# Two weight remainders and the output matrix of a decode step, loaded with source runs that span several written rows

## The chip, the cores and the metric

The kernel runs on one core of a Trainium2 chip. The metric is device time in microseconds (us) of one execution. All matrices come from HBM and are read once into SBUF, the core's on-chip memory of 128 partitions; the result goes back to HBM. The core has five instruction queues: TensorE (PE, matrix multiply, with weight loads listed as PEld), VectorE (DVE), ScalarE (ACT), GpSimd (POOL) and SyncE (SP). In this kernel SP issues every transfer, and one hardware queue (q1 in the profile) spreads each of them over the core's 16 DMA engines.

## What is computed

Eight tokens (B = 8, one position each, D = 576) pass through two branches, which a sigmoid gate mixes. The inputs are bfloat16.

```python
g = sigmoid((x * gate_w).sum(-1, keepdims=True))
# a: attention of 32 query heads over 16 key/value heads, the last W = 2048 positions of the caches
q = x @ wq                                             # wq: 576 x 4096
p = softmax(einsum(q, k[:, :, Sk-W:]) * 128 ** -0.5)
a = einsum(p, v[:, :, Sk-W:]).reshape(B, 1, 4096) @ wo # wo: 4096 x 576
# b: layernorm and a two-layer network
h = gelu(layernorm(x) @ w1 + b1)                       # w1: 576 x 4608
b = h @ w2 + b2                                        # w2: 4608 x 576
out = g * a + (1 - g) * b
```

The windows of the two caches are 2 x 67.1 MB; wq, w1, w2 and wo are 4.7, 5.3, 5.3 and 4.7 MB.

## The kernel before, in words

**An order made by a planner.** The kernel registers every operation with an engine, its dependencies, an estimated cost and a priority (`add` and `dma`, line 50 and below). `_Plan.schedule` (line 62) then lays out one order for each engine from these estimates; `emit` writes it out with semaphore waits for the dependencies. On each engine, and on SP, instructions run in that fixed order. An `after=` dependency fixes order alone and makes no wait.

**The buffers.** `RAW` holds four slots of 32 KB a partition, and behind them a fifth, shorter one (number `ND` = 4, 18 KB a partition). The fifth shares its bytes with `KT2`, a work buffer of transposed keys (line 280). `take_slot` (line 606) deals out slots 1, 2, 0, 3 in turn; `slot_free[s]` lists who must have finished reading slot `s` before it is filled again.

**The stream.** First come wq and w1. Each has 576 rows and is split into 512 rows, four to a partition (`d_wqm`, `d_w1m`), and a remainder of 64 rows (`d_wqr`, `d_w1r`, lines 407 and 417), in which each row is cut in two halves so that the 128 halves fill 128 partitions: 4096 bytes a partition for wq, 4608 for w1. Then 16 items of keys and 16 of values follow, 4 MB each (`load_item`, line 613, issued at line 618): 128 partitions of 32 KB, where a source item of one batch and head gives four consecutive partitions. Behind the last value item come w2 and wo:

```python
M_CUTS = [[24], [8, 3, 1]]
stream += [("M", 0), ("W", 0), ("W", 1), ("M", 1)]
```

`M` 0 is 24 of the 36 column blocks of w2 in one transfer (3456 KB), `M` 1 the other 12 in three transfers of 8, 3 and 1 blocks (1152, 432 and 144 KB; `m2_chunk`, issued at line 865). `W` 0 and 1 are the two halves of wo (2304 KB each, 18,432 bytes a partition; `wo_chunk`, line 832, issued at line 836). `W` 0 goes to slot ND and so waits for the last matmuls that read `KT2`, those of the last key item; `W` 1 and both `M` go to slots from `take_slot`. What each waits for: `M` 0 the third-last value item's matmuls, `W` 1 the last key item's transposes, `M` 1 the second-last value item's matmuls.

**Who uses them.** `AccGroup` (line 570) makes the matmuls of the two final products, all at line 579. They add into one PSUM bank; every 576-column block is done as two matmuls of 288 columns, on different parts of the array. `m2_…` groups multiply with w2 and need only hT, the hidden layer, which is ready early. `proj0` and `proj1` multiply with wo and need `oT`, the finished attention output (line 822), whose last part comes from the last value item by way of a short matmul group (`sel_x`, line 819). Between `proj0` and `proj1` stands `fill`: eight matmuls of 512 columns whose result nobody reads (`filler`, line 846, matmuls at line 851 and in the helper at line 175). Groups are tied to each other by `after=`, so that their order in PE's queue follows the stream. At the end VectorE and ScalarE each copy half of the accumulator (lines 900 and 901), and SP writes the output (line 903).

## Time and profile before

| | |
|---|---|
| Device time, median of 3 runs | 364.61 us (364.40 to 364.72) |
| Span of the profiled execution, first to last instruction | 363.0 us (its own total is not shown apart; the runs are about 1.6 us longer than the span) |
| Mean granted TensorE clock | 0.958 of full speed |
| TensorE / VectorE / ScalarE busy | 82% / 64% / 46% of the span |
| Bytes read from HBM | 154.29 MB |
| DMA engines busy with q1 | 98.8% of the span, 16 engines |
| Transfers under 8 KB a packet | 1228 of 6102 packets |

The profile's page gives busy shares, then the span in 40 slices, the DMA queues, and the chain that ended last: the work followed back from the last instruction, at each step to whatever released it. Further views used below are that chain in order of time, the timeline of one engine, the waits, the DMA queue in a stretch of time, and a table of stretches with the busy time of each engine and the granted TensorE clock. Busy time of SP (SPq) is the time in which it issues a transfer; the transfer itself runs long after that.

### The profile page before, as it was taken

To read this page: it belongs to the slowest core of one execution; us is meant where nothing else is said; L and a number is where in the kernel's file an instruction comes from. 1 tells how busy PE (TensorE), PEld (TensorE's weight loads), DVE (VectorE), ACT (ScalarE), POOL (GpSimd) and SP (SyncE) were. 2 spreads that over 40 slices of the span, in tenths; PEclk is the share of its full clock that TensorE was granted. 3 is DMA by queue.
4 is the path that set the end of the run, shared out by engine and by line. 5 is a ranking of instruction groups with operands and counts; after the bars stand their busy time and mean duration, and the time that the engine had idled before them with its cause. 6 is when DMAs were issued, how large, how long until landed. Compare 5 with 4: busy or idle time off the path is not lost.

```text
span 363.0 us, 4821 instructions
## 1 busy us (share of the span) xinstructions
PE 297.9 (82%) x1954; PEld 125.3 (35%) x1423; DVE 231.4 (64%) x166; ACT 168.6 (46%) x130; POOL 22.9 (6%) x52
## 2 busy tenths in 40 slices
PE   0456366999999979998897979997989698999875
PEld 0111000434252615242433417150615152436742
DVE  0452989576666694929385768566675949295720
ACT  1022106656647463663637373838374554656000
POOL 9032030000010000000100000000000000003000
PEclk9976598999999998999999989999999999999999
DMA  8999999999999999999999999999999999999996
GB/s 347 436 437 406 455 412 455 412 455 412 450 415 451 415 451 413 441 426 441 426 441 426 435 430 437 430 437 428 437 430 437 430 435 430 437 430 433 415 430 257
DMA packets 6102, 154.45 MB, mean 426 GB/s; under 512 B 694, under 2 KB 840, under 8 KB 1228
## 3 DMA queue, kind: packets, MB, share of 16 engines
q1 hardware_dynamic: 6092, 154.30, 98.8%
q8 instruction: 8, 0.13, 0.1%
q14 instruction: 2, 0.02, 0.0%
HBM read 154.29 MB, written 0.01 MB: 425 GB/s over the span
## 4 chain that ended last, share of the span: by engine, by line
DMA 56%; DVE 27%; PE 14%; issue 1%; ACT 1%; SPq 0%; POOL 0%
DMA arena<-in_A_k_cache_dram 47%; DVE arena L718 21%; PE ps L175 6%; DMA arena<-in_B_w_dram 6%; DMA arena<-in_A_x_dram 3%; DVE arena L668 2%; PE ps L188 2%; PE ps L755 2%; PE ps L732 2%; DVE arena L645 1%; PE ps L501 0%; PE ps L579 0%; DVE arena L557 0%; DVE arena L521 0%; ACT arena L536 0%
## 5 line engine op out<-in xcount | busy, mean ns | idle before, releaser
L718 DVE STREAM_TRANSPOSE arena<-arena 128x4096 f32<-128x4096 f32 (+1 forms) x34 | 141.7, 4175 | 21.9 <-DMA arena<-in_A_k_cache_dram 21.9
L674 ACT ACTIVATE arena<-arena 32x2048 bf16<-32x2048 bf16 x60 | 114.5, 1908 | 71.4 <-DVE arena L668 42.9
L175 PE MATMUL ps<-arena 128*128 128x512 bf16 (+3 forms) x531 | 136.1, 402 | 0.0
L188 PE MATMUL ps<-arena 128*128 x840 | 109.5, 277 | 7.3 <-issue 1.2
L188 PEld LDWEIGHTS ps<-arena 128*128 x840 | 81.4, 97 | 34.3 <-issue 19.0
L732 PE MATMUL ps<-arena 128*128 128x512 bf16 x128 | 51.4, 401 | 27.6 <-DVE arena L718 26.1
L645 DVE TENSOR_REDUCE arena<-ps 128x1 f32<-128x2048 f32 x16 | 36.7, 2291 | 53.8 <-PE ps L175 53.8
L732 PEld LDWEIGHTS ps<-arena 128*128 128x128 bf16 x128 | 12.5, 98 | 131.7 <-issue 75.3
L649 ACT ACTIVATE arena<-ps,arena 128x2048 bf16<-128x2048 f32 x16 | 40.7, 2543 | 0.5
L646 ACT ACTIVATE arena<-arena 128x1 f32<-128x1 f32 x16 | 3.2, 203 | 63.5 <-DVE arena L645 63.5
L755 PE MATMUL ps<-arena 128*128 128x256 bf16 x184 | 25.3, 272 | 1.1 <-DVE arena L663 1.1
L755 PEld LDWEIGHTS ps<-arena 128*128 128x128 bf16 x184 | 16.9, 99 | 18.8 <-issue 14.6
L668 DVE STREAM_TRANSPOSE arena<-arena 128x1024 f32<-128x1024 f32 x15 | 18.1, 1205 | 2.9 <-ACT arena L649 2.9
L579 PE MATMUL ps<-arena 128*8 128x288 bf16 (+1 forms) x140 | 9.6, 286 | 4.0 <-DMA arena<-in_A_wo_dram 3.3
L739 POOL MEMSET arena<- 128x4096 f32 x1 | 3.5, 3511 | 148.2 <-PE ps L175 148.2
L685 PE MATMUL ps<-arena 128*128 128x512 bf16 x16 | 6.5, 407 | 6.5 <-ACT arena L649 5.2
L629 POOL COPY arena<-arena 32x64 bf16<-32x64 bf16 x16 | 3.7, 229 | 123.3 <-PE ps L175 122.4
L901 ACT ACTIVATE arena<-ps 8x288 bf16<-8x288 f32 x1 | 0.4, 402 | 19.5 <-PE ps L579 19.5
L422 DVE COPY arena<-arena 8x128 bf16<-8x128 bf16 x2 | 0.5, 228 | 13.9 <-DMA arena<-in_A_x_dram 13.9
L579 PEld LDWEIGHTS ps<-arena 128*8 128x8 bf16 (+1 forms) x140 | 5.8, 86 | 9.9 <-DMA arena<-in_A_wo_dram 3.3
L900 DVE CAST arena<-ps 8x288 bf16<-8x288 f32 x1 | 0.4, 446 | 12.3 <-PE ps L579 12.3
L557 DVE TENSOR_TENSOR arena<-arena 128x1152 f32<-128x1152 f32 x1 | 1.4, 1358 | 9.7 <-ACT arena L555 9.7
(106 smaller groups left out, 94.0 us busy)
## 6 DMA issues: line engine op xcount, KB each, us to landing
arena<-in_A_k_cache_dram SPq DMA_DIRECT2D x16, 4096.0 KB, 28.7
arena<-in_A_v_cache_dram SPq DMA_DIRECT2D x16, 4096.0 KB, 25.5
arena<-in_B_w_dram SPq DMA_DIRECT2D x1, 4608.0 KB, 22.0
arena<-in_A_wo_dram SPq DMA_DIRECT2D x2, 2304.0 KB, 23.8
arena<-in_A_wq_dram SPq DMA_DIRECT2D x1, 4096.0 KB, 12.6
arena<-in_B_w_dram SPq DMA_DIRECT2D x1, 3456.0 KB, 24.1
arena<-in_B_w_dram SPq DMA_DIRECT2D x1, 1152.0 KB, 22.3
arena<-in_B_w_dram SPq DMA_DIRECT2D x1, 576.0 KB, 23.0
```

The costliest lines, as they stand in the source:

```text
L175: return e.add_instruction(mybir.InstMatmult(name=nc.get_next_instruction_name(), engine=mybir.EngineType.PE, ins=[e.lower_ap(rhs), e.lowe ...
L188: return e.add_instruction(mybir.InstMatmult(name=nc.get_next_instruction_name(), engine=mybir.EngineType.PE, ins=[rhs, lhsT], outs=[e.low ...
L579: ins = e.matmul(ps[32 * j:32 * j + 8, BK_ACC, 0:JN], lhsT, rhs[:, JN * j:JN * j + JN], start=False, stop=True, skip_group_check=True, til ...
L629: return e.tensor_copy(dst, src)
L645: mx = add("dve", lambda e: e.tensor_reduce(out=k(g, MX + x), in_=scores, axis=AXL.X, op=ALU.max), deps=[qk_unit[t]], name="mx%d" % t, cos ...
L649: ex = add("act", lambda e: e.activation(out=bass.AP(arena, offset=aoffs("P"), ap=[[AST, 128], [64, 32], [1, 2], [2, 32]]), in_=ps[:, 0:4, ...
L668: pc = add("dve", lambda e: e.transpose(view("PC").bitcast(F32), view("P").bitcast(F32)), deps=[ex] + (sp_done[t - 1][0] if t else [o_acc0 ...
L674: return e.activation(out=bass.AP(arena, offset=32 * a * AST + aoffs(home) + 64 * a, ap=[[AST, 32], [256, 32], [1, 64]]), in_=bass.AP(aren ...
L685: mm = e.matmul(*args, start=True, stop=False, skip_group_check=True) if n == 0 else held_matmul(nc, e, *args, start=True, stop=False, ski ...
L718: return e.transpose(bass.AP(arena_f, offset=foffs(base) + 2048 * h0, ap=[[AST // 2, 128], [1, 2048 * nh]]), bass.AP(arena_f, offset=foffs ...
L732: mm = e.matmul(*args, start=False, stop=True, skip_group_check=True) if rc == 0 else held_matmul(nc, e, *args, stop=True, skip=True)
L755: return e.matmul(dst, bass.AP(arena, offset=aoffs(home) + 256 * q + ee, ap=[[AST, 128], [2, 128]]), slot(s).rearrange("p (r k d) -> p r k ...
```

## The change

A new helper, `wide_read`, issues a DMA copy whose two sides have different shapes but the same elements in the same order. Three loads use it.

The remainders of wq and w1 are now described on the HBM side as 16 runs of four whole rows (32,768 bytes for wq, 36,864 for w1), and on the SBUF side as before, 128 rows of 4096 or 4608 bytes: one run fills eight partitions. The bytes land in the same places.

The two halves of wo become one transfer of 128 runs of 36,864 bytes on the HBM side; each run fills two rows of 18,432 bytes in the same partition, one in the slot that `take_slot` gives and one in slot ND. The transfer therefore waits for both slots. The stream's tail is now wo, `M` 0, `M` 1, so wo takes the slot that `M` 0 had, and `M` 0 the one that `W` 1 had. Both `proj` groups wait for the one transfer; `fill` stands behind `proj1`. In PE's order `proj0`, `proj1` and `fill` come first, and all of `M` 0's 48 matmuls behind them; before, 32 of these stood ahead of `sel_x`, 16 behind it, and all 48 ahead of `proj0`. No other instruction changes its place on any engine.

```diff
+def wide_read(nc, e, dst, src):
+    return e.add_instruction(mybir.InstDMACopy(
+        name=nc.get_next_instruction_name(), engine=mybir.EngineType.SP, queue="qSPDynamicHW", mode="Copy",
+        ins=e.lower_ap_dma(src), outs=e.lower_ap_dma(dst), oob_is_err=True, cce_op=ALU.bypass))
...
-        d_wqr = dma("sp", lambda e: e.dma_start(wq_r, A_wq[512:576, :].rearrange("k (s c) -> (k s) c", s=2)), "wq", 64 * 8192, name="d_wqr")
+        d_wqr = dma("sp", lambda e: wide_read(nc, e, wq_r, A_wq[512:576, :].rearrange("(q k) c -> q (k c)", k=4)), "wq", 64 * 8192, name="d_wqr")
...
-        d_w1r = dma("sp", lambda e: e.dma_start(w1_r, B_w1[512:576, :].rearrange("k (s c) -> (k s) c", s=2)), "w1", 64 * F * 2, name="d_w1r", after=[d_w1m])
+        d_w1r = dma("sp", lambda e: wide_read(nc, e, w1_r, B_w1[512:576, :].rearrange("(q k) c -> q (k c)", k=4)), "w1", 64 * F * 2, name="d_w1r", after=[d_w1m])
...
-        stream += [("M", 0), ("W", 0), ("W", 1), ("M", 1)]
+        stream += [("W", 0), ("M", 0), ("M", 1)]
...
-        def wo_chunk(i):
-            s = ND if i == 0 else take_slot()
-            dst = slot(s)[:, 0:WOR * D].rearrange("p (j c) -> p j c", j=WOR)
-            src = A_wo.rearrange("(p j) c -> p (j c)", j=WOP)[:, WOR * D * i:WOR * D * (i + 1)]
-            d = dma("sp", lambda e: e.dma_start(slot(s)[:, 0:WOR * D], src), "s%d" % s, WOR * 128 * D * 2, deps=slot_free[s], name="d_wo%d" % i, after=last_dma[-1:])
-            last_dma.append(d)
-            mms = [(oT[:, WOR * i + j, :], dst[:, j, :]) for j in range(WOR)]
-            slot_free[s] = [AccGroup("proj%d" % i, mms, [oT_done[n] for n in range(NG)] + [d], cost=2.4, prio=2, after=o_m2[-1:]).op]
-            o_m2.append(slot_free[s][0])
-            if i == 0:
-                filler("fill", 8, o_m2[-1:])
+        def wo_both():
+            s = take_slot()
+            homes = (s, ND)
+            dst = bass.AP(arena, offset=aoffs("RAW") + s * DE, ap=[[AST, 128], [(ND - s) * DE, 2], [1, WOR * D]])
+            src = A_wo.rearrange("(p j) c -> p (j c)", j=WOP).unsqueeze(1)
+            d = dma("sp", lambda e: wide_read(nc, e, dst, src), "s%d" % ND, WOP * 128 * D * 2, deps=slot_free[ND] + slot_free[s], name="d_wo", after=last_dma[-1:])
+            last_dma.append(d)
+            for i, h in enumerate(homes):
+                mms = [(oT[:, WOR * i + j, :], slot(h)[:, j * D:(j + 1) * D]) for j in range(WOR)]
+                slot_free[h] = [AccGroup("proj%d" % i, mms, [oT_done[n] for n in range(NG)] + [d], cost=2.4, prio=2, after=o_m2[-1:]).op]
+                o_m2.append(slot_free[h][0])
+                if i == 1:
+                    filler("fill", 8, o_m2[-1:])
...
-            {"K": k_item, "V": v_item, "W": wo_chunk, "M": m2_chunk, "B": bias}[kind](i)
+            {"K": k_item, "V": v_item, "W": lambda i: wo_both(), "M": m2_chunk, "B": bias}[kind](i)
```

## The prediction

> **What bounds the kernel now.** I read the page's queue rows first, since every byte is read once: if the queue is full from end to end, only transfer time and the two ends count.

> ```profile
> span 363.0 us, 4821 instructions
> DMA  8999999999999999999999999999999999999996
> q1 hardware_dynamic: 6092, 154.30, 98.8%
> ```

> The DMA digits are 9 in all slices but the first and the last, and q1 keeps 16 engines at 98.8% of the span. So whatever lengthens or shortens a transfer moves the end by as much. The second view is the chain that ended last, in order of time.

> ```profile
> 1.71 12.15 DMA arena<-in_A_x_dram
> ...
> 79.66 25.41 DMA arena<-in_A_k_cache_dram
> ...
> 337.03 22.31 DMA arena<-in_B_w_dram
> ...
> 359.38 1.71 PE ps L579 x24
> ...
> 361.12 0.45 DVE arena L900
> ```

> From 79.66 us on it is nearly all waiting for key transfers; at the end it is the 1152 KB piece of w2, 24 matmuls, the copy out. The tail, where the change reorders work, I read in the timeline of all engines.

> ```profile
> 345.67 2.13 PE L579 MATMUL ps<-arena 128*8 128x288 bf16 x32
> ...
> 347.73 0.19 PE L819 MATMUL ps<-arena 128*128 128x32 bf16 x1
> ...
> 348.33 0.44 DVE L822 TENSOR_TENSOR arena<-ps,arena 128x64 bf16<-128x64 f32 x1 [0.92 <-PE ps L175]
> 351.23 2.13 PE L579 MATMUL ps<-arena 128*8 128x288 bf16 x32 [1.85 <-DMA arena<-in_A_wo_dram]
> ...
> 353.29 0.39 PE L851 MATMUL ps<-arena 128*128 128x512 bf16 x1
> 353.51 1.67 PE L175 MATMUL ps<-arena 128*128 128x512 bf16 x7
> 356.65 2.13 PE L579 MATMUL ps<-arena 128*8 128x288 bf16 x32 [1.46 <-DMA arena<-in_A_wo_dram]
> ...
> 359.38 1.70 PE L579 MATMUL ps<-arena 128*8 128x288 bf16 x24 [0.61 <-DMA arena<-in_B_w_dram]
> ```

> PE takes each weight transfer as it lands: `M` 0 at 345.67, the halves of wo at 351.23 and 356.65, `M` 1 from 359.38. Between the pieces it idles, since the queue is slower than PE. Each of these gaps will matter.

> **The change part by part.** The sum is made on the profiled span, 363.0 us; the runs (median 364.61) lie 1.6 us above it, and a difference is carried over as it is.

> *Fewer, longer reads.* How the time of a packet depends on its size comes from two stretches of the queue: one of key and value rows of 32,768 bytes, one of mostly 9216-byte rows.

> ```profile
> DMA packets 1493, 43.23 MB, mean 432 GB/s; under 512 B 172, under 2 KB 172, under 8 KB 172
> ...
> q1 hardware_dynamic: 1490, 43.19, 100.1%
> ```
> ```profile
> DMA packets 74, 0.61 MB, mean 380 GB/s; under 512 B 8, under 2 KB 8, under 8 KB 8
> ...
> q1 hardware_dynamic: 74, 0.61, 89.7%
> ```

> In the first, 432 GB/s at 100.1% busy is 27.0 bytes/ns for one engine, 1215 ns for a 32 KB packet. In the second, 66 packets above 512 B hold 0.61 MB, 9242 bytes each, at 380/0.897 = 424 GB/s: 349 ns each. The slope is 866 ns over 23,526 bytes, 36.8 ps a byte, which leaves some 9 ns that a packet costs whatever its size. The remainders have 8 rows on each engine (128/16); with one read for eight rows, 7 x 9 = 63 ns go, twice. wo goes from 16 packets on an engine to 8: 72 ns. Together 0.2 us, if the 9 ns belong to the read; if they belong to the written row, nothing. I take 0.18, since the rows count one packet for a read and a write, and keep 0 as the other end. Longer runs do not move faster otherwise: wo's rows already have half the length.

> *Issuing.* The three copies leave the short form of issue.

> ```profile
> 0.80 0.39 SPq L407 DMA_DIRECT2D arena<-in_A_wq_dram  x1
> ...
> 282.81 0.54 SPq L618 DMA_DIRECT2D arena<-in_A_v_cache_dram  x1
> ...
> 321.52 0.33 SPq L865 DMA_DIRECT2D arena<-in_B_w_dram  x1
> 329.90 0.81 SPq L836 DMA_DIRECT2D arena<-in_A_wo_dram  x2
> 337.03 1.28 SPq L865 DMA_DIRECT2D arena<-in_B_w_dram  x3
> ```

> The wq remainder took 0.39 us to issue; key and value loads, whose two sides also differ in shape, 0.54. The queue is empty behind the first load, so its 0.15 us more is on the path: +0.15 (0 if it issues as before). For the other two the queue is full when they issue.

> *wo waits for two slots.* SP's wait at line 836 was 8.0 us, for the last key item's matmuls, until 329.90. Before, `M` 0 had gone out at 321.52; now wo goes first and stands until 329.9, with both `M` behind it.

> ```profile
> SPq L836 <- PE ps L175: 8.0, 1, 8.0
> ```
> ```profile
> arena<-in_B_w_dram SPq DMA_DIRECT2D x1, 3456.0 KB, 24.1
> arena<-in_A_wo_dram SPq DMA_DIRECT2D x2, 2304.0 KB, 23.8
> ```

> What hides this is the last value item. `M` 0 landed at 345.67, and 3456 KB at 432 GB/s are 8.2 us, so the value item moves until 337.5. An issue at 329.9 leaves 7.6 us of cover: cost nothing. Without the cover it would be 8 us. `M` 0 is issued right behind, `M` 1 at 337.03 as before (its wait is unchanged, and 19 us of bytes stand ahead of it).

> *The tail in the new order.* wo is 4608 KB: 10.9 us, landed at 348.4. `sel_x` no longer stands behind `m2` matmuls (until 347.80 before), so oT is ready no later than its 348.77, rather at 348.5; `proj` starts at about 348.6. The 64 `proj` matmuls go in pairs, two parts of the array at once:

> ```profile
> L579 PE MATMUL ps<-arena 128*8 128x288 bf16 (+1 forms) x140 | 9.6, 286 | 4.0 <-DMA arena<-in_A_wo_dram 3.3
> ```

> 32 of them took 2.13 us, one lasts 0.286: 15 steps in 1.84 us, 0.1225 us a pair. So `proj` ends at 348.6 + 32 x 0.1225 = 352.5, and `fill` (353.29 to 355.18 before, 1.9 us) at 354.4. The bytes up to the end of `M` 0 are those that ended with wo before, so `M` 0 lands where the second half of wo did, at 356.6. Then 48 + 24 matmuls are still to do, 36 pairs: the last starts at 356.65 + 35 x 0.1225 = 360.94 and ends at 361.22. Before, the end was 361.08, set by landings (`M` 1's first piece at 359.34, the last one 24 matmuls of 1.71 us later). So PE, not the last landing, ends the kernel: +0.15 us (361.22 for 361.08), at full clock.

> *The clock in that tail.* PE now idles from 354.4 to 356.6, 2.2 us; before from 355.18 to 356.65, 1.46. What a gap of that size does shows in mid-kernel, in the table of stretches (its length, then busy us and instructions of PE, PEld, DVE, ACT and POOL, granted clock, DMA share, GB/s):

> ```profile
> 131.68:135.10 3.42, 1.45 (x7) 0.10 (x1) 3.42 (x1) 3.37 (x3) 0.00 (x0) 1.00 1.04 450
> 135.10:138.51 3.41, 3.16 (x8) 0.40 (x3) 1.23 (x5) 2.60 (x2) 0.00 (x0) 0.50 1.02 442
> 189.70:193.11 3.41, 1.72 (x9) 0.10 (x1) 2.78 (x1) 3.36 (x3) 0.00 (x0) 1.00 1.03 442
> 193.11:196.53 3.42, 3.42 (x19) 0.73 (x8) 0.18 (x1) 2.99 (x3) 0.00 (x0) 1.00 0.95 412
> 353.55:356.96 3.41, 1.95 (x14) 0.25 (x8) 0.00 (x0) 0.00 (x0) 0.00 (x0) 1.00 0.94 400
> 356.96:360.38 3.42, 2.81 (x46) 1.76 (x42) 0.00 (x0) 0.00 (x0) 0.00 (x0) 1.00 0.76 307
> ```
> ```profile
> 132.30 0.84 PE L175 MATMUL ps<-arena 128*128 128x512 bf16 x3
> 135.35 0.61 PE L732 MATMUL ps<-arena 128*128 128x512 bf16 x1 [2.22 <-DVE arena L718]
> 135.76 1.48 PE L175 MATMUL ps<-arena 128*128 128x512 bf16 x3
> ```

> The granted clock changes in steps of 3.41 us. A stretch in which PE was busy 1.45 of 3.42 us (42%, one gap of 2.22) is followed by one at 0.50, in which three matmuls spread over 1.48 us instead of 0.84; a stretch with 1.72 busy (50%) is followed by full clock. So the limit lies between 42 and 50%. From 135.10 on, 64 steps of 3.413 lead to 353.5. In the stretch 353.55 to 356.96 PE was busy 1.95 us (57%). In the new order it holds `fill` until 354.4 and matmuls from 356.6: 1.2 us, 36%. Then 356.96 to 360.38 runs at half clock, and 3.41 us there do 1.7 us of work. The end is 1.7 us later.

> [...]

> If the steps lie elsewhere in another execution, the drop comes when a step holds at least 1.7 to 2.0 us of the 2.2-us gap, and not when PE had already been slowed at 348 (the new hole between 345.6 and 347.5), which lengthens `proj` and closes the gap: by these times a third to a half of the positions.

> Sum: +0.15 issue, −0.18 packets, +0.15 PE at the end, +1.7 half clock = +1.8: 364.61 + 1.8 = 366.4 us.

> **The rivals.** *The tail stays at full clock.* The same sum without the last term: +0.1, 364.7 us. For it: steps in another place, or `fill` a little later (wo landing 0.5 us later than reckoned moves `fill` so that the stretch is over 50% busy). Against it: the place of the steps in this trace.

> *Two engines write into one part of SBUF.* A key or value item gives four consecutive partitions and moves at 432 GB/s although its two sides have unequal outer counts (32 and 128). A new run gives eight. If an engine's eight rows then cross into the part of SBUF that another engine fills at that time, each has half the rate, and the remainders (0.52 + 0.59 MB, 2.6 us at 432 GB/s) take up to twice as long: +1.3 if half of it collides, +2.6 at most; 364.61 + 0.1 + 2.4 = 367.1 us. Nothing in the trace shows a written run of eight partitions, and the full rate of the key loads speaks against it. wo is not touched: its 128 runs stay in their partitions.

> [...]

> *Faster.* The start is slow:

> ```profile
> DMA packets 106, 0.43 MB, mean 310 GB/s; under 512 B 0, under 2 KB 0, under 8 KB 106
> ...
> q1 hardware_dynamic: 106, 0.43, 87.8%
> ```

> In the first 1.4 us the queue moves 310 GB/s instead of 432: 0.4 us lost, and the first packet cannot start before 1.8. If one long read for each engine closes this, the issue is not longer, all 0.2 us of packets go, and PE stays at full clock: −0.4 −0.2 +0.15 = −0.45. It decides, over 0.2%, when a further 0.3 us come from less spread between engines at the end: 363.8 us.

> *The change does not do what it says:* the queue may cut the runs into row-sized packets again. Then the 0.18 stays, and with it the tail: 366.6, or 364.9 at full clock. It changes no sign and goes with those cases.

> **How the numbers follow.** About 0.2%, 0.7 us, is what a measurement of this kernel can tell from no change. Half clock in the tail: 0.36 (the profiled place of the steps gives it surely, a free place in a third to a half). Full clock and no collision: 0.29. Collision: 0.24. Faster by over 0.2%: 0.11. So slower 0.60, same 0.29, faster 0.11. The predicted time is that of the first, 366.4; its own range is 366.0 to 366.8. The range for all reaches from 364.2 (full clock, some of the start gained) to 367.8 (collision with its 2.6 us and some spread); below it lies faster, above it collision and half clock together (up to 369).

> **What would show it.** Packets of 32 KB and more in place of the 256 of 4096 and 4608 bytes; the wq remainder's issue at 0.54; wo landed near 348.4; `fill` ended near 354.4 and PE idle until 356.6; a granted clock of 0.50 in a stretch that begins between 356 and 358.3, with the last 72 matmuls at 0.245 us a pair. The prediction is wrong if the clock stays at 1.00 there; a collision would show as a later landing of x (before, the chain waits for it until 13.86) and of everything behind it, at an unchanged rate in the key loads.

## The result

The changed kernel takes 366.94 us (median of 4 runs, 366.58 to 367.04) against 364.61 us, a ratio of 1.0063 with a 95% interval of 1.005 to 1.0077: 2.3 us slower. The spans of its four executions are 365.3 to 365.4 us; the profiled one before was 363.0. The forecast was 366.4 us, with a range of 364.2 to 367.8. The number came out, but most of it from another cause than the one I had put first; that 366.4 lies so near to 366.94 is luck. One execution in the whole record, the third of `e10` (400.16 us, not traced), lies far above the others of its kernel and is left out of the comparisons.

**The profile after.** First the page: span, DMA engines and rate in 40 slices, packets of the whole run.

```profile
span 365.3 us, 4801 instructions
DMA  8999999999999999999999999999999999999995
GB/s 298 419 401 436 405 456 405 456 409 456 414 443 434 427 452 411 449 413 449 416 452 416 443 427 434 441 423 447 413 449 416 452 414 445 423 438 445 408 437 240
DMA packets 5734, 154.45 MB, mean 423 GB/s; under 512 B 678, under 2 KB 824, under 8 KB 956
```

For comparison, the rate row of the kernel before:

```profile
GB/s 347 436 437 406 455 412 455 412 455 412 450 415 451 415 451 413 441 426 441 426 441 426 435 430 437 430 437 428 437 430 437 430 435 430 437 430 433 415 430 257
```

The packets fell from 6102 to 5734: 224 for the remainders, 128 for wo, and 16 of the small ones (under 512 B: 678 after, 694 before; there is one transfer fewer, but what these packets carry no view says). So the long runs are really read as such. The queue is as full as before (DMA digits of 9), but it moves less in the first three slices: 298 for 347 GB/s, 419 for 436 and 401 for 437. In the first the remainder of wq is loaded, in the third that of w1 begins. From the fourth slice on, up to the last, both rows swing between about 405 and 456.

Next the transfers that matter here, picked from the list, with their size and the time from issue to landing, first after, then before:

```profile
arena<-in_B_w_dram SPq DMA_DIRECT2D x1, 4608.0 KB, 22.5
arena<-in_A_wo_dram SPq DMA_DIRECT2D x1, 4608.0 KB, 18.5
arena<-in_B_w_dram SPq DMA_DIRECT2D x1, 576.0 KB, 24.6
arena<-in_A_wq_dram SPq DMA_DIRECT2D x1, 512.0 KB, 4.6
```
```profile
arena<-in_B_w_dram SPq DMA_DIRECT2D x1, 4608.0 KB, 22.0
arena<-in_B_w_dram SPq DMA_DIRECT2D x1, 576.0 KB, 23.0
arena<-in_A_wq_dram SPq DMA_DIRECT2D x1, 512.0 KB, 3.3
```

And the issues at the start in the timeline of SP (start, duration), after and then the two of w1 before:

```profile
0.80 0.62 SPq L196 DMA_DIRECT2D arena<-in_A_wq_dram  x1
1.49 0.56 SPq L414 DMA_DIRECT2D arena<-in_A_wq_dram  x1
3.65 0.36 SPq L422 DMA_DIRECT2D arena<-in_B_w_dram  x1
4.05 0.52 SPq L196 DMA_DIRECT2D arena<-in_B_w_dram  x1
```
```profile
3.23 0.36 SPq L416 DMA_DIRECT2D arena<-in_B_w_dram  x1
3.63 0.43 SPq L417 DMA_DIRECT2D arena<-in_B_w_dram  x1
```

The 512 KB of wq, issued first, land 4.6 us after the issue for 3.3. The main part of w1 was issued at 3.23 before and at 3.65 now, so it lands at 3.65 + 22.5 = 26.15 for 3.23 + 22.0 = 25.23: 0.9 later. The w1 remainder lands at 4.05 + 24.6 = 28.65 for 3.63 + 23.0 = 26.63: 2.0 later, another 1.1. From there to the last transfer the shift hardly grows, as the chain that ended last shows (start, duration; its first transfer and its end):

```profile
4.61 35.08 DMA arena<-in_A_k_cache_dram
332.74 26.02 DMA arena<-in_B_w_dram
358.80 4.60 PE ps L585 x72
```

`M` 0 lands at 332.74 + 26.02 = 358.76. The forecast put it where the second half of wo had landed, at 356.6; it is 2.2 later, and the end is 2.3 later. So nearly the whole loss was made in the first 29 us. The rate in between is unchanged: 434 GB/s from 140 to 240 us, 432 before.

Last the tail, in PE's timeline (lines picked out) and in the table of stretches (columns as in the prediction: length, busy us of PE, PEld, DVE, ACT, POOL, granted clock, DMA share, GB/s):

```profile
344.17 3.65 PE L761 MATMUL ps<-arena 128*128 128x256 bf16 x32
349.70 0.19 PE L825 MATMUL ps<-arena 128*128 128x32 bf16 x1 [1.88 <-DVE arena L814]
350.82 5.32 PE L585 MATMUL ps<-arena 128*8 128x288 bf16 x64 [0.53 <-DVE arena L828]
356.29 1.67 PE L175 MATMUL ps<-arena 128*128 128x512 bf16 x7 [0.16 <-issue]
358.80 4.58 PE L585 MATMUL ps<-arena 128*8 128x288 bf16 x72 [0.83 <-DMA arena<-in_B_w_dram]
```
```profile
346.54:349.96 3.42, 1.54 (x22) 1.17 (x16) 1.64 (x5) 0.00 (x0) 0.00 (x0) 1.00 0.92 396
349.96:353.37 3.41, 2.88 (x35) 1.60 (x28) 0.44 (x1) 0.00 (x0) 0.00 (x0) 0.50 1.03 446
353.37:356.78 3.41, 3.25 (x49) 1.85 (x41) 0.00 (x0) 0.00 (x0) 0.00 (x0) 1.00 0.94 399
356.78:360.20 3.42, 2.59 (x30) 1.04 (x26) 0.00 (x0) 0.00 (x0) 0.00 (x0) 1.00 0.94 399
360.20:363.61 3.41, 3.18 (x52) 2.10 (x48) 0.19 (x1) 0.19 (x1) 0.00 (x0) 1.00 0.45 178
```

The chain ends with 72 matmuls right behind `M` 0's landing, as forecast, but they take 4.58 us at a granted clock of 1.00. The half-clock stretch is there, only earlier: PE idles from 347.8 to 349.7, waiting for attention's last part; the stretch from 346.54 is 45% busy; the next one runs at 0.50. The 64 `proj` matmuls stretch to 5.32 us, `fill` ends at 358.0, and of the 2.2-us gap ahead of the last 72 matmuls 0.83 us remain. The clock drop fell on work that has slack: the last 72 matmuls wait for `M` 0 all the same.

### The profile page after: what moved, and what is told of

It reads as the page before. It is cut to its first block, busy times and chain, and to the rows that moved or that the text cites. A ratio compares the mean times of both kernels' runs of the same rounds, so it can differ in the third digit from the quotient of the medians.

```text
span 365.3 us, 4801 instructions
## 1 busy us (share of the span) xinstructions
PE 296.5 (81%) x1935; PEld 126.0 (34%) x1423; DVE 231.5 (63%) x166; ACT 168.6 (46%) x130; POOL 23.0 (6%) x52
## 2 busy tenths in 40 slices
DMA packets 5734, 154.45 MB, mean 423 GB/s; under 512 B 678, under 2 KB 824, under 8 KB 956
## 3 DMA queue, kind: packets, MB, share of 16 engines
q1 hardware_dynamic: 5724, 154.30, 98.6%
## 4 chain that ended last, share of the span: by engine, by line
DMA 55%; DVE 22%; PE 20%; SPq 1%; issue 1%
DMA arena<-in_A_k_cache_dram 48%; DVE arena L724 18%; PE ps L175 9%; DMA arena<-in_B_w_dram 7%; PE ps L188 6%; PE ps L738 3%; DVE arena L674 2%; PE ps L585 1%; DVE arena L651 1%; DVE arena L800 1%; PE ps L761 0%; SPq L196 0%; PE ps L691 0%; SPq L414 0%; DVE arena L908 0%
## 5 line engine op out<-in xcount | busy, mean ns | idle before, releaser
L175 PE MATMUL ps<-arena 128*128 128x512 bf16 (+3 forms) x524 | 134.6, 397 | 13.5 <-DVE arena L724 10.6
L738 PE MATMUL ps<-arena 128*128 128x512 bf16 x122 | 48.7, 399 | 19.0 <-DVE arena L724 17.3
L761 PE MATMUL ps<-arena 128*128 128x256 bf16 x184 | 25.3, 273 | 1.2 <-DVE arena L669 1.1
L428 DVE COPY arena<-arena 8x128 bf16<-8x128 bf16 x2 | 0.5, 228 | 15.2 <-DMA arena<-in_A_x_dram 15.2
L691 PE MATMUL ps<-arena 128*128 128x512 bf16 x11 | 4.4, 399 | 5.2 <-ACT arena L655 5.2
L908 DVE CAST arena<-ps 8x288 bf16<-8x288 f32 x1 | 0.4, 445 | 12.7 <-PE ps L585 12.7
## 6 DMA issues: line engine op xcount, KB each, us to landing
arena<-in_B_w_dram SPq DMA_DIRECT2D x1, 4608.0 KB, 22.5
arena<-in_B_w_dram SPq DMA_DIRECT2D x1, 3456.0 KB, 26.0
arena<-in_B_w_dram SPq DMA_DIRECT2D x1, 576.0 KB, 24.6
```

Of the source, the lines that this page charges most:

```text
L175: return e.add_instruction(mybir.InstMatmult(name=nc.get_next_instruction_name(), engine=mybir.EngineType.PE, ins=[e.lower_ap(rhs), e.lowe ...
L691: mm = e.matmul(*args, start=True, stop=False, skip_group_check=True) if n == 0 else held_matmul(nc, e, *args, start=True, stop=False, ski ...
L738: mm = e.matmul(*args, start=False, stop=True, skip_group_check=True) if rc == 0 else held_matmul(nc, e, *args, stop=True, skip=True)
L761: return e.matmul(dst, bass.AP(arena, offset=aoffs(home) + 256 * q + ee, ap=[[AST, 128], [2, 128]]), slot(s).rearrange("p (r k d) -> p r k ...
```

## The experiments

Each kernel is compared with executions of the kernel before from the same round (medians 364.45 to 364.58 us, median span 363.0 in each). The theory after the result: the two remainders cost about 1 us each because of their runs of eight written rows (that these collide in SBUF was a conjecture, and no view shows it); the tail costs 0.15 us; the half clock did not reach the end. The rivals: the loss comes from the long reads as such, from the longer issue, or from the new tail.

**One part at a time.** Three kernels take one part of the change each: `e1` the wq remainder, `e2` the w1 remainder, `e3` wo with the tail's new order (all the lines of the diff that are not `d_wqr` or `d_w1r`).

```diff
 e1:
-  e.dma_start(wq_r, A_wq[512:576, :].rearrange("k (s c) -> (k s) c", s=2))
+  wide_read(nc, e, wq_r, A_wq[512:576, :].rearrange("(q k) c -> q (k c)", k=4))
 e2:
-  e.dma_start(w1_r, B_w1[512:576, :].rearrange("k (s c) -> (k s) c", s=2))
+  wide_read(nc, e, w1_r, B_w1[512:576, :].rearrange("(q k) c -> q (k c)", k=4))
 e3:
-        stream += [("M", 0), ("W", 0), ("W", 1), ("M", 1)]
+        stream += [("W", 0), ("M", 0), ("M", 1)]
...
+            d = dma("sp", lambda e: wide_read(nc, e, dst, src), "s%d" % ND, WOP * 128 * D * 2, deps=slot_free[ND] + slot_free[s], name="d_wo", after=last_dma[-1:])
```

> Only the wq remainder is read in runs of eight written rows; w1 and wo as before. Theory (two engines write into one part of SBUF while an engine's share is eight neighbouring partitions): the wq weights land about 1.1 us later than before, as in the changed kernel (14.96 for 13.88 us), and the time is 365.5 to 365.8. Rival (the loss is in the issue and start of the first load alone): 364.8, 0.2 us more. Rival (the loss is in the tail): 364.6.

> Only the w1 remainder is read in runs of eight written rows. Theory (shared part of SBUF): the w1 remainder lands 1.0 to 1.1 us later, time 365.6 to 365.8. Rival (issue and start of the first load): 364.6, since this load is not first. Rival (tail): 364.6.

> Only wo in one transfer, with the new order of the tail; both remainders as before. Theory (shared part of SBUF): wo's runs stay in their own partitions, so no loss in the transfer; PE ends the kernel 0.15 us later and 8 packets an engine go: 364.6 to 364.8, and in an execution whose last stretch is at half clock 366.3. Rival (long reads that fill several rows are slow in themselves): wo, with 4.7 MB, loses more than the remainders did with 1.1 MB, several us.

Measured: the wq remainder alone 365.37 us, ratio 1.0022 (1.0013 to 1.0032), span 364.0; the w1 remainder alone 365.54 us, 1.0024 (1.0015 to 1.0034), span 364.1. By the medians of the spans (363.85 and 364.1, before 363.0) the first costs 0.85 us and the second 1.1, so that about 2.0 of the 2.3 us are thereby placed. wo alone took 365.57 us, 1.0023 (1.0007 to 1.0039), but its six spans fall into two groups, 363.1 to 363.6 and 364.7 to 364.8. The profiled execution is of the second group; its transfer of wo, its PE timeline and its stretches:

```profile
arena<-in_A_wo_dram SPq DMA_DIRECT2D x1, 4608.0 KB, 18.4
```
```profile
348.53 4.09 PE L585 MATMUL ps<-arena 128*8 128x288 bf16 x64 [0.53 <-DVE arena L828]
352.77 1.67 PE L175 MATMUL ps<-arena 128*128 128x512 bf16 x7
356.52 6.25 PE L585 MATMUL ps<-arena 128*8 128x288 bf16 x72 [2.07 <-DMA arena<-in_B_w_dram]
```
```profile
353.46:356.87 3.41, 1.34 (x11) 0.27 (x8) 0.00 (x0) 0.00 (x0) 0.00 (x0) 1.00 0.91 386
356.87:360.29 3.42, 3.42 (x34) 1.91 (x30) 0.00 (x0) 0.00 (x0) 0.00 (x0) 0.50 0.77 310
```

This is the tail of the forecast almost to the digit: `proj` from 348.5, `fill` ended at 354.4, PE idle for 2.07 us, `M` 0 landed at 356.5, the stretch from 353.46 busy for 1.34 of 3.41 us (39%), and 0.50 in the stretch from 356.87. The 72 matmuls take 6.25 us for the 4.58 of full clock: 1.67 us lost, where I had worked out 1.7. What the two groups of spans are is read from this one trace and from the size of the step between them, 1.1 to 1.7 us; the executions of the lower group were not traced.

**Long reads, or the grouping?** `e6` is the kernel before with its short reads of 4096 and 4608 bytes, and only describes the source of both remainders as 16 groups of eight rows in place of 128 rows.

```diff
-  e.dma_start(wq_r, A_wq[512:576, :].rearrange("k (s c) -> (k s) c", s=2))
+  wide_read(nc, e, wq_r.unsqueeze(1), A_wq[512:576, :].rearrange("(q k) (s c) -> q (k s) c", k=4, s=2))
...
-  e.dma_start(w1_r, B_w1[512:576, :].rearrange("k (s c) -> (k s) c", s=2))
+  wide_read(nc, e, w1_r.unsqueeze(1), B_w1[512:576, :].rearrange("(q k) (s c) -> q (k s) c", k=4, s=2))
```

> [...] Theory (shared part of SBUF): as slow as the two remainders of the changed kernel, +2.0 to +2.2, 366.6 to 366.8. Rival (the long read itself is slow): 364.6 to 364.9, since no read is longer than before.

The transfers and the page's packet row of that kernel:

```profile
DMA packets 6102, 154.45 MB, mean 423 GB/s; under 512 B 694, under 2 KB 840, under 8 KB 1228
```
```profile
arena<-in_B_w_dram SPq DMA_DIRECT2D x1, 576.0 KB, 24.9
arena<-in_A_wq_dram SPq DMA_DIRECT2D x1, 512.0 KB, 4.6
```

366.84 us, ratio 1.0067 (1.0047 to 1.0088); three of its four spans are 365.2 to 365.4, one, not traced, is 366.4. With the packets of the kernel before, the remainders take 4.6 and 24.9 us, nearly as in the changed kernel (4.6 and 24.6), and wo and the tail, which are as before here, make no difference that shows. So the length of the reads costs nothing that shows; the description in 16 groups of eight rows brings the loss. Part of it is a later start: the first load takes 0.68 us to issue, longer than the 0.39 before, and how much that costs the next runs show.

**Groups of four rows.** `e4` is the changed kernel with two source rows to a run, 32 runs of four written rows; `e5` and `e12` put the same into the kernel before, `e5` in both remainders, `e12` in that of w1 alone.

```diff
-  wide_read(nc, e, wq_r, A_wq[512:576, :].rearrange("(q k) c -> q (k c)", k=4))
+  wide_read(nc, e, wq_r, A_wq[512:576, :].rearrange("(q k) c -> q (k c)", k=2))
...
-  wide_read(nc, e, w1_r, B_w1[512:576, :].rearrange("(q k) c -> q (k c)", k=4))
+  wide_read(nc, e, w1_r, B_w1[512:576, :].rearrange("(q k) c -> q (k c)", k=2))
```

> The changed kernel, but a run of the two remainders is two rows long (32 runs, four written rows each) instead of four rows (16 runs, eight written rows). Theory (an engine's eight neighbouring partitions collide): a run of four partitions is what a key item has, so the 2.0 us of the two remainders go; wq lands at 13.9 to 14.1 again, and what is left is the tail of the run with wo alone: 364.6 to 366.4 by execution, median near 365.4. Rival (reads that fill several written rows are slow in themselves): still 1 us or more over the run with wo alone.

> The kernel before, with the two remainders in runs of two rows (four written rows each); wo and the tail untouched. Theory (collision): no loss, and at most 0.1 us of packets gained, less the longer issue of the first load (0.15 to 0.25 us): 364.4 to 364.8. Rival (reads that fill several written rows are slow): 365.4 or more.

> The kernel before, with the w1 remainder alone in runs of two rows. The run with both remainders in runs of two rows was 0.35 us slower. If that was the first load's longer issue, this run equals the kernel before, 364.5 to 364.7, since its load is not first. If reads that fill several written rows cost something, +0.15 us or more: 364.7 to 364.9.

`e4`: 365.07 us, 1.0021 (1.0009 to 1.0033); nine of eleven spans are 363.4 to 363.9, two, not traced, are 365.0 and 365.5, as far apart as the groups of `e3`. `e5`: 364.91 us, 1.001 (1.000 to 1.0019). `e12`: 364.59 us, 1.0003 (0.9994 to 1.0012). The transfers of `e12` and the first issues of `e5`:

```profile
arena<-in_B_w_dram SPq DMA_DIRECT2D x1, 576.0 KB, 23.1
```
```profile
0.80 0.56 SPq L196 DMA_DIRECT2D arena<-in_A_wq_dram  x1
1.42 0.56 SPq L414 DMA_DIRECT2D arena<-in_A_wq_dram  x1
```

With four written rows to a run the loss of 1 us is gone: the w1 remainder takes 23.1 us from its issue, before 23.0. But nothing is gained either: three quarters of the packets of that transfer are saved, and no time. What is left in `e5`, 0.3 us by the median of its spans (363.3 for 363.0), is its first load: it issues for 0.56 us instead of 0.39, and the load behind it for 0.56 instead of 0.41. `e12`, which leaves the first load as it was, is level with the kernel before (median span 363.0).

**Does the loss grow with the bytes?** The 512 KB of the remainder are too little to tell a start-up cost from a rate. `e10` is the kernel before with the 4 MB part of wq described as 16 groups of eight rows, with unchanged packets of 32 KB.

```diff
-  e.dma_start(wq_m.rearrange("p t c -> p (t c)"), A_wq[0:512, :].rearrange("(p t) c -> p (t c)", t=4))
+  wide_read(nc, e, RAW[:, 0:4 * 4096].unsqueeze(1), A_wq[0:512, :].rearrange("(q p t) c -> q p (t c)", p=8, t=4))
```

> [...] Theory (pairs of engines write one part of SBUF while another stands idle): the loss grows with the bytes. Eight rows at 1.21 us each are 9.7 us for an engine; engines that start together would lose up to as much again, some less by the spread of their starts: wq lands 6 to 9.7 us later, time 371 to 374. Rival (a fixed cost for each transfer described in 16 groups): about 1 us, 365.4 to 365.8, as for the remainders, whose bytes are an eighth.

376.06 and 376.92 us, ratio 1.0331 (1.0312 to 1.035). That transfer (12.6 us before), and the queue in the stretch in which it moves, beside the same stretch of the kernel before:

```profile
arena<-in_A_wq_dram SPq DMA_DIRECT2D x1, 4096.0 KB, 25.3
```
```profile
DMA packets 171, 4.28 MB, mean 218 GB/s; under 512 B 29, under 2 KB 39, under 8 KB 43
```
```profile
DMA packets 171, 4.24 MB, mean 438 GB/s; under 512 B 30, under 2 KB 40, under 8 KB 44
```

The same 171 packets move at 218 GB/s in place of 438: half, for as long as the transfer lasts. The transfer ends 12.7 us later than before (25.3 us from issue for 12.6), more than the 6 to 9.7 I had expected; the small load of x, issued behind it, releases VectorE at 24.24 us for 13.89, 10.35 later. So the cost is a rate, and of the forms tried here (one, four or eight consecutive partitions to a group) it is halved only with eight (218 GB/s, against 438 with one and the 432 of the key items with four). Two things stay untested. All these transfers fill 128 partitions, so groups of eight are also 16 groups and groups of four are 32: the number of groups was not varied apart from their size. And no view shows which rows of HBM one engine reads, or where it writes them, so no run tells a collision in SBUF from one at HBM.

**The clock in the tail.** `e8` runs the changed kernel again. `e9` is `e3` with a `fill` of 16 matmuls, to keep PE busy up to `M` 0. `e11` adds to that seven filling matmuls ahead of `sel_x`, in the hole from 345.6 to 347.5; nobody reads the results of any of these.

```diff
 e9, against e3:
-                    filler("fill", 8, o_m2[-1:])
+                    filler("fill", 16, o_m2[-1:])
 e11, beside that (the second line shortened; the new `after=` fixes order alone):
+                if g == NG - 1:
+                    filler("fill0", 7, pe_hist[-1:])
+                sx = add("pe", sel_x, ..., after=o_m2[-1:] if g == NG - 1 else [], prio=3 if g == NG - 1 else 0)
```

> The changed kernel, unchanged, for more executions. If the clock of the last 72 matmuls falls in a third to a half of the executions, as in the run with wo alone, some of these have a span near 367.0 beside those at 365.3 to 365.4; if the place of the clock's steps is tied to the kernel's start, all stay at 365.3.

> The run with wo alone, with 16 instead of 8 filling matmuls behind the products with wo, which then end at about 356.3, just before the large piece of w2 lands at 356.5. If the gap of 2.1 us is what drops the clock, no execution has the last 72 matmuls at half clock, and all times lie within 0.3 us at 364.6 to 364.9. If the clock falls for another reason, the times spread from 364.5 to 366.4 as before.

> wo in one transfer with the tail's order, as in the run with wo alone, but seven filling matmuls ahead of the short group behind the last value item, and 16 instead of 8 behind the products with wo, so that PE has no gap over 1 us from 341 to 357. If the two gaps are what drops the clock, no execution drops it, the last matmul ends about 0.15 us later than before and the times lie within 0.4 us near 364.7. If something else drops it, spans spread from 363.0 to 364.8 again.

`e8`: 366.73 us, 1.0058 (1.0044 to 1.0072), five spans from 365.2 to 365.5, no second group. `e9`: 365.45 us, 1.0017 (1.0008 to 1.0026); spans 363.0 to 363.3 five times, 363.8 to 364.3 six times. `e11`: 364.50 us, 1.0002 (0.9993 to 1.0011), spans 362.9 to 363.6. PE's timeline in the three kernels, in this order:

```profile
350.92 5.76 PE L585 MATMUL ps<-arena 128*8 128x288 bf16 x64 [0.53 <-DVE arena L828]
358.82 4.58 PE L585 MATMUL ps<-arena 128*8 128x288 bf16 x72 [0.32 <-DMA arena<-in_B_w_dram]
```
```profile
348.76 5.40 PE L585 MATMUL ps<-arena 128*8 128x288 bf16 x64 [0.53 <-DVE arena L828]
354.32 3.40 PE L175 MATMUL ps<-arena 128*128 128x512 bf16 x15 [0.16 <-issue]
357.65 4.58 PE L585 MATMUL ps<-arena 128*8 128x288 bf16 x72
```
```profile
349.12 4.09 PE L585 MATMUL ps<-arena 128*8 128x288 bf16 x64 [0.53 <-DVE arena L830]
357.09 4.58 PE L585 MATMUL ps<-arena 128*8 128x288 bf16 x72 [0.33 <-DMA arena<-in_B_w_dram]
```

The stretch of `e8` ahead of its drop and the one of `e11` that holds most of its last 72 matmuls:

```profile
347.60:351.01 3.41, 1.00 (x22) 0.59 (x13) 2.08 (x6) 0.00 (x0) 0.00 (x0) 1.00 0.83 357
```
```profile
357.46:360.87 3.41, 3.41 (x60) 2.53 (x56) 0.00 (x0) 0.00 (x0) 0.00 (x0) 1.00 0.72 289
```

In `e8`, too, the drop came early, on `proj` (5.76 us), behind a stretch that was 29% busy, and left 0.32 us of the gap. In `e9` no traced matmul of the last 72 is slow, as expected, but the mend costs time itself: when the earlier hole slows `proj` to 5.40 us, the long `fill` ends at 357.7 and, since `M` 0 landed at 356.5, holds the last 72 matmuls back by about 1 us. This half of the expectation failed: a filler has to be shorter than the slack in the slowest case. With both holes filled (`e11`) the clock stays at 1.00 to the end, `proj` takes 4.09 us, and wo in one transfer is level with the kernel before. No version is faster than the kernel before beyond what a measurement can tell.

How busy PE has to be for the clock to hold doesn't come out as one number. Two stretches, each with the one behind it, first of `e10`, then of `e2`:

```profile
360.01:363.43 3.42, 1.69 (x34) 1.08 (x24) 0.45 (x1) 0.00 (x0) 0.00 (x0) 1.00 1.03 436
363.43:366.84 3.41, 3.31 (x28) 1.88 (x30) 0.00 (x0) 0.00 (x0) 0.00 (x0) 0.50 0.98 419
```
```profile
212.03:215.45 3.42, 1.43 (x7) 0.19 (x2) 2.97 (x5) 3.37 (x3) 0.00 (x0) 1.00 0.93 402
215.45:218.86 3.41, 3.41 (x35) 1.48 (x19) 1.07 (x2) 0.95 (x1) 0.00 (x0) 1.00 1.02 442
```

In `e10` PE was busy 1.69 of 3.42 us (49%) and the clock fell; in `e2` it was busy 1.43 (42%) and the clock held. In `e10` the idle time stands at the end of the stretch, in `e2` at its start. So between these shares the busy share alone doesn't tell what the clock does next; what else decides stays open.

## Why the prediction was right, and which step failed

- *The queue bounds the kernel.* Right: what the remainders lost by 28.65 us (2.0 us) was still there when `M` 0 landed at 358.76 (2.2 us).
- *The collision*, "Two engines write into one part of SBUF", stood as a rival at 0.24 with 367.1 us, +1.3 to +2.6 for both remainders. A loss of that size and form is what happened: +0.85 for wq, some 0.3 of it from the longer start, and +1.1 for w1 (`e1`, `e2`, `e5`, `e6`, the half rate in `e10`). Its signs were seen too: x lands at 15.2 instead of 13.86, and the rate of the key and value items behind it is unchanged (434 GB/s, before 432). I set it low because the key loads, with unequal sides like these, move at the full 432 GB/s. That argument went by the wrong feature: the key loads write runs of four partitions, and `e4`, `e5` and `e12` show that four are free (the w1 remainder in `e12`: 23.1 us from issue to landing, before 23.0); eight are not (24.6). Why, the runs don't show: neither which engine writes which partitions nor that engines meet in SBUF at all. The collision itself, and a share of eight neighbouring partitions for each engine, with which the expectations reckon, were my assumptions; what the runs show is the rate, 218 GB/s for 438 in `e10`.
- *The half clock, +1.7*, the largest term of the sum, is the step that failed. The prediction named its own sign of being wrong, a clock of 1.00 in the stretch that begins between 356 and 358.3, and that is what was seen: the stretch from 356.78 ran at 1.00, and the last 72 matmuls took 4.58 us. What stood in its place is the loss of about 2.0 us in the two remainders. Without the remainders the step comes as forecast, in mechanism and size, in the traced execution of `e3` (2.07 us of gap, 39%, 1.67 us lost), but its place was worked out for a tail that starts at 348.6. The slower remainders moved the tail by 2.2 us, while the clock's steps happen to lie in the profiled run almost where they lay before (346.54, before 353.55 − 2 x 3.41 = 346.72). So the hole ahead of `sel_x`, which a step would have cut in two, fell into a single stretch, and the drop came on `proj`. In `e8` the steps lie 1.1 us later, and the drop came on `proj` as well. I had named this case ("lengthens `proj` and closes the gap"), but had not seen that the collision and the half clock depend on each other; I added them for the case above the range ("up to 369") as if they were free.
- *The limit for the clock, "between 42 and 50%"*, was read from one trace and is not a limit of the busy share alone: 49% was followed by half clock in `e10`, 42% by full clock in `e2` (both shown above). The 36% that the prediction reckoned with lie below that band, the 45% ahead of the early drop inside it.
- *Packets, −0.18.* Not confirmed. From the landing of the last value item to that of `M` 0 the queue took 19.09 us after and 19.11 before; over all traces it is 19.02 to 19.11 with wo in one transfer and 18.90 to 19.17 with wo in two, so that the 0.07 forecast for wo can't be told from nothing. The w1 remainder in the four-row form saved 0.02 us on average, with overlapping spreads (1.35 to 1.38 us, 1.37 to 1.40 before), where 9 ns a packet would give 0.05.
- *Issue, +0.15.* Too small: 0.23 for the first load and 0.15 more for the one behind it, which I had not charged. With four written rows to a run, where nothing else is lost, this start costs 0.3 us by the spans (363.3 for `e5`, 363.0 for `e12` and before); the interval of `e5`, 1.000 to 1.0019, reaches down to no change.
- *wo's wait for two slots, 0.* Right: `e3` issued at 329.86 and landed 18.4 us later, at 348.3; forecast 348.4.
- *The tail at full clock, +0.15.* In line with what was seen: the lower spans of `e3` (363.1 to 363.6) and those of `e11` (362.9 to 363.6) against 363.0. The end is set by PE, as forecast.
- *That the queue cuts the runs again* did not happen (5734 packets).

The sum that did happen: +0.85 for wq (with its longer start), +1.1 for w1, +0.15 in the tail, 0 for packets and clock: +2.1, measured +2.3. The 0.2 left over is not placed.

**Open.** In none of the nine executions of the changed kernel do the spans (365.2 to 365.5) leave room for 1.7 us of half clock at the end; two were traced, and both had the early drop. With three of six in `e3`, and two of eleven in `e4` if its two long spans are the same, one would expect some among nine if the steps lay at any place with equal chance; by these shares together, 5 of 17, none in nine has a chance of about 4%. In the 13 traces of this case the places of the steps, carried by multiples of 3.413 us to one spot of the span, cover 2.3 of the 3.4 us; whether they are partly tied to the start of the kernel was not settled. Nor was it settled why the transfers in groups of eight lose half their rate (218 for 438 GB/s), in SBUF or at HBM.

## What to carry to other kernels

When a transfer's source is described in fewer, longer runs, count the partitions that one run fills: here, with four the key items moved at 432 GB/s and the w1 remainder lost nothing (23.1 us from issue to landing for 23.0), with eight the 4 MB of wq had half their rate (218 for 438 GB/s), and the w1 remainder took 24.6 us with long reads, 24.9 with short ones. The queue here, already full with packets of 4 KB and more, gained nothing measurable from longer ones (1.35 to 1.38 us for the w1 remainder in the four-row form, 1.37 to 1.40 before). And in these tails the clock fell to 0.50 behind 3.41-us stretches in which PE was 29 to 49% busy, that is, idle for 1.7 to 2.4 us; whether that hurts depends on whether the next work has slack, so look at every hole in a tail, and at a delay's effect on all of them, before adding terms.
